# The last projection of 1024 tokens by Strassen's seven products, with the operand sums made during the gate stage

## The chip, the cores and the metric

The kernel runs on one core of one Trainium2 chip. The metric is the device time of one execution in microseconds (us). All runs told here are fast, at a granted TensorE clock of 0.996 to 1.0. In the profile lines PE is TensorE, PEld its weight loads, DVE VectorE, ACT ScalarE, POOL GpSimd and SPq the queue that issues the stores. PSUM is the memory of the tiles that matmuls write here, SBUF that of the other tiles in the kernel. A ratio of two kernels is the mean time of one kernel's fast runs over the mean of the other's of the same rounds, so it is not quite the ratio of the medians that are quoted.

Single executions of the same kernel here differ by up to 5 us. The text therefore uses a second measure, read from the traces: **the stage time, from the start of the first matmul of the second gate stage to the end of the span**. Everything that this study changes, but for a data type and the place of two loads of `x1` in the stages before, lies inside that stretch. The page gives spans to 0.1 us, so a difference of less than 0.1 us means nothing here.

## The reference

```python
def _B_ref(x, w_in, w_sp, b_sp, w_out):          # S = 2048 tokens, D = 1024, Fh = 1792
    z = gelu(einsum('bsd,df->bsf', x, w_in))
    z1 = z[..., :Fh]
    z2 = layernorm(z[..., Fh:])
    g = einsum('ts,bsf->btf', w_sp, z2) + b_sp[None, :, None]
    return einsum('bsf,fd->bsd', z1 * g, w_out)
...
h = layernorm(x) * (1 + ca) + sa
x = x + ga * attention(h)                        # "x1" in the kernel
h = layernorm(x) * (1 + cb) + sb
x = x + gb * _B_ref(h, ...)                      # the last line is what the change touches
```

The work at issue is `x1 + gb * ((z1 * g) @ w_out)` for the second 1024 tokens: a product of 1024 x 1792 with 1792 x 1024.

## The kernel before

Most large products of the kernel are already done by Strassen's scheme: a 2 x 2 block product in seven products instead of eight. A `Block` holds one such product. TensorE accumulates products 1, 6, 5 and 3 one after the other in the same PSUM bank `a`, and a "snap" of the running sum is taken before the next product is added. Products 2, 7 and 4 have the banks `c` and `b`.

```python
class Block:
    BANK = {1: "a", 6: "a", 5: "a", 3: "a", 2: "c", 7: "b", 4: "b"}
    ...
    def finish(self, n):
        ps = self.ps[self.BANK[n]]
        if n == 1:   self.s = self.snap(ps, 1)
        elif n == 2: self.out(1, 1, ps, self.s)
        elif n == 6: self.x = self.snap(ps, 2)
        elif n == 5: self.out(2, 2, self.ps["b"], self.snap(ps, 3))
        elif n == 3: self.out(1, 2, ps, None)
        elif n == 4: self.out(2, 1, ps, self.x)
        ...                                   # hooks: work to issue after product n

def steady(prev, blocks):                     # products 3 and 4 of a block run inside the next block
    for b in blocks:
        for n in (1, 2, 3, 6, 7, 4, 5):
            if n in (3, 4):
                prev and prev.run(n)
            else:
                b.run(n)
        prev = b
    return prev
```

The gate stage multiplies by `w_sp` in seven blocks for each half of the tokens, one for each pair of 128-feature groups. Its result `g` is multiplied into `z1T` by VectorE. The last projection is plain: 14 matmuls for each 128 tokens x 512 columns.

```python
def project(ti):
    ...
    cuts = (0, 512, D) if ti < NT - 1 else (0, 512, 768, 896, D)
    for c0, c1 in zip(cuts, cuts[1:]):
        bo = bank_ps("bo", [P, 512])[:, 0:c1 - c0]
        for f in range(NF):                                       # NF = 14
            nc.tensor.matmul(bo, z1T[ti // 8, f // 2][:, f % 2, t0:t0 + P],
                             wout[f // 2][:, f % 2, sl], start=(f == 0), stop=(f == NF - 1))
        nc.vector.tensor_mul(out=t, in0=bo, in1=late_gb[0][:, sl])
        nc.vector.tensor_add(out=outt[:, sl], in0=t, in1=x1rs[ti][:, sl])
        ...                                                       # store to the output
...
prev = steady(None, gates[1])        # the second gate stage
prev.run(3)
prev.run(4)
for ti in range(8, NT):              # the last projection
    project(ti)
```

The softmax here doesn't subtract the row's maximum and nothing guards it: scores larger than these inputs give would overflow.

Of the kernel before, what the change touches and what calls it, by code (L numbers as in the profile page):

```python
# [9 lines left out]
BF16 = mybir.dt.bfloat16  # L10
FP16 = mybir.dt.float16
# [5 lines left out]
def kernel(  # L17
# [16 lines left out]
    nc = tc.nc  # L34
    P = 128
    D = 1024
    S = 2048
    NT = 16
# [19 lines left out]
    def wide_ps(name, shape=(P, 1024), dtype=FP32):  # L58
        return psum.tile(list(shape), dtype, name=name, tag="wide", bufs=2)

    def bank_ps(name, shape, dtype=FP32):
        return psum.tile(shape, dtype, name=name, tag="bank", bufs=3)
# [23 lines left out]
    out_dram = out[0].rearrange("(tt p) d -> p tt d", p=P)  # L86
# [63 lines left out]
    cols = early.tile([P, 2, KD], FP32, name="cols")  # L150
# [234 lines left out]
    first = q_work(0, 0, bank_ps, outs)  # L385
# [56 lines left out]
    heap = Heap()  # L442
# [153 lines left out]
    for g, (i, kb) in enumerate(steps):  # L596
# [41 lines left out]
        n = (FILL if i else FILL0)[kb]  # L638
        if kb == 0:
            n = n if i + 1 < len(halves) else 1  # L640
# [3 lines left out]
            n = 0  # L644
        for j in range(2):
            nc.tensor.matmul(o_ps[j][:], vs[h][:, kb, :], pt[:, j * 512:(j + 1) * 512],  # L646
                             start=(kb == 0), stop=(kb == NKB - 1))
# [17 lines left out]
        elif kb == 14 and i + 2 == len(halves):  # L665
# [4 lines left out]
                stop=(k == 15), skip_group_check=True) for k in range(16)]  # L670
        if i + 1 == len(halves) or (i + 2 == len(halves) and kb >= 14):
            n = 1
# [20 lines left out]
    def scratch(name, shape, dtype=FP32):  # L693
        return scr.tile(shape, dtype, name=name, tag="k2", bufs=11)

    def short(name):
        return scr.tile([P, 512], FP16, name=name, tag="k1", bufs=6)
# [3 lines left out]
    def after(n, fn):  # L701

        later.append([n, fn])
# [54 lines left out]
    def steady(prev, blocks):  # L758
# [8 lines that stand above are left out]
# [28 lines left out]
    def copy_snap(ps, which):  # L795
        t = scratch("snap", [P, 512])[:, 0:ps.shape[1]]
        nc.scalar.activation(t, ps, ACT.Copy)  # L797
        return t

    def add_to(ps, snap):  # L800
        t = scratch("sum", [P, 512])[:, 0:ps.shape[1]]
        nc.vector.tensor_add(out=t, in0=ps, in1=snap)  # L802
        return t
# [171 lines left out]
    def h_op(c, m):  # L975
        return {1: hT[c, 0, 0], 2: hT[c, 0, 1], 4: hT[c, 1, 1], 3: hs[c][4], 5: hs[c][1],
                6: hs[c][2], 7: hs[c][3]}[m]
# [20 lines left out]
    w1, w1t, z1T = {}, {}, {}  # L998
# [51 lines left out]
    prev = steady(wos[3], wos[4:])  # L1050

    def gelu(dst, ps, snap):
        if snap is None:
            nc.scalar.activation(dst, ps, ACT.Gelu_apprx_tanh)
        else:
            t = add_to(ps, snap)
            after(2, lambda: nc.scalar.activation(dst, t, ACT.Gelu_apprx_tanh))
# [10 lines left out]
    def done_with_h(c):  # L1068
        users[c] -= 1
        if not users[c]:  # L1070
            heap.give(*(hT[c, i, j] for i in range(2) for j in range(2)),
                      *(hs[c][n] for n in (1, 2, 4)))
# [54 lines left out]
    def z1_block(c, p):  # L1127
        def operands(n):
            h = h_op(c, n)
            b = {1: (0, 0), 2: (1, 0), 3: (1, 1)}.get(n)  # L1130
            if b:
                w = [w1[c, p][:, 4 * b[0] + dc, b[1] * P:(b[1] + 1) * P] for dc in range(4)]
            else:
                w = [w1t[c, p][:, {4: 3, 5: 0, 6: 1, 7: 2}[n], dc, :] for dc in range(4)]
            return w, [h[:, dc, :] for dc in range(4)]

        def out(i, j, ps, snap):
            if (c, p) not in z1T:
                z1T[c, p] = heap.take("z1T", [P, 2, 1024], BF16)
            gelu(z1T[c, p][:, j - 1, (i - 1) * 512:i * 512], ps, snap)  # L1140

        b = Block(operands, copy_snap, out)
        b.on(3, lambda: done_with_h(c))
        return b
# [3 lines left out]
    NG = NF // 2  # L1148
    WQ = ((0, 1), (1, 1), (0, 0), (1, 0))
    W, wb, zr, zs, bb = {}, {}, {}, {}, {}  # L1150
# [55 lines left out]
    def zq(c, p, k, i):  # L1206
        return zr[c, p, k][:, :, i * P:(i + 1) * P]

    def z_sum(c, p, m):

        a11, a21, a12, a22 = (zq(c, p, k, i) for k in range(2) for i in range(2))
        if m == 1:
            zs[c, p] = heap.take("zs", [P, 2, 8, P], FP16)
            nc.vector.tensor_add(out=zs[c, p][:, 0], in0=a21, in1=a22)
        elif m == 2:
            nc.vector.tensor_sub(out=zs[c, p][:, 1], in0=zs[c, p][:, 0], in1=a11)
        elif m == 3:
            nc.vector.tensor_sub(out=a21, in0=a11, in1=a21)
        else:
            nc.vector.tensor_sub(out=a12, in0=a12, in1=zs[c, p][:, 1])  # L1220
# [3 lines left out]
    def work(n=1):  # L1224
        def go():
            for _ in range(n):
                if tasks:
                    tasks.pop(0)()
        return go
# [9 lines left out]
    for n, s in enumerate(seq):  # L1239
        b = z1b[n]  # L1240
# [29 lines left out]
    prev = dual(prev, order)  # L1270


    def plus(out, ps, other):
        nc.vector.scalar_tensor_tensor(out=out, in0=ps, scalar=DOWN, in1=other,  # L1274
                                       op0=ALU.mult, op1=ALU.add)

    def gate_block(c, p):
        def operands(n):
            if n in (5, 6):
                lhs = [zs[c, p][:, n - 5, k, :] for k in range(8)]  # L1280
            else:
                k_, i = {1: (0, 0), 7: (0, 1), 2: (1, 0), 3: (1, 0), 4: (1, 1)}[n]
                lhs = [zq(c, p, k_, i)[:, k, :] for k in range(8)]
            return lhs, [wb[n, k // 4][:, k % 4, :] for k in range(8)]

        def b(j):
            return bb[c][:, (j - 1) * 512:j * 512]

        def snap(ps, which):
            t = scratch("snap", [P, 512])  # L1290
            plus(t[:], ps, b({1: 1, 2: 1, 3: 2}[which]))
            return t[:]

        def out(i, j, ps, other):
            g = short("g").bitcast(BF16)
            plus(g[:], ps, b(2) if other is None else other)
            z = z1T[c, p][:, i - 1, (j - 1) * 512:j * 512]
            nc.vector.tensor_mul(out=z, in0=z, in1=g[:])

        g = Block(operands, snap, out)  # L1300
        g.on(2, lambda: z_sum(c, p, 4))
        g.on(7, lambda: heap.give(zr.pop((c, p, 0))))
        g.on(5, lambda: heap.give(zs.pop((c, p))))
        g.on(4, lambda: heap.give(zr.pop((c, p, 1))))
        if p + 1 < NG:
            g.on(1 if p else 2, lambda: norm_z(c, p + 1, 0))
            g.on(7, lambda: z_sum(c, p + 1, 1))
            g.on(5, lambda: z_sum(c, p + 1, 3), lambda: z_sum(c, p + 1, 2))
        if p + 2 < NG:
            g.on(7, lambda: load_z(c, p + 2, 0))  # L1310
            g.on(5, lambda: norm_z(c, p + 2, 1))
        if p + 3 < NG:
            g.on(4, lambda: load_z(c, p + 3, 1))
        return g

    wout, late_gb = {}, []
# [8 lines left out]
    x1rs = {}  # L1325

    def load_x1(ti):
        x1rs[ti] = scratch("x1r", [P, D], BF16)
        nc.sync.dma_start(x1rs[ti][:], x1_dram[ti])

    def project(ti):
        if ti + 2 < NT:
            load_x1(ti + 2)
        outt = scratch("outt", [P, D], BF16)
        cuts = (0, 512, D) if ti < NT - 1 else (0, 512, 768, 896, D)
        t0 = (ti % 8) * P
        for c0, c1 in zip(cuts, cuts[1:]):
            sl = slice(c0, c1)
            bo = bank_ps("bo", [P, 512])[:, 0:c1 - c0]
            for f in range(NF):  # L1340
                nc.tensor.matmul(bo, z1T[ti // 8, f // 2][:, f % 2, t0:t0 + P],  # L1341
                                 wout[f // 2][:, f % 2, sl], start=(f == 0),
                                 stop=(f == NF - 1))
            t = scratch("t", [P, 512])[:, 0:c1 - c0]
            nc.vector.tensor_mul(out=t, in0=bo, in1=late_gb[0][:, sl])  # L1345
            nc.vector.tensor_add(out=outt[:, sl], in0=t, in1=x1rs[ti][:, sl])
            if ti == NT - 1:
                nc.sync.dma_start(out_dram[:, ti, sl], outt[:, sl])
            work(2)()
        if ti < NT - 1:  # L1350
            nc.sync.dma_start(out_dram[:, ti, :], outt[:])

    gates = [[gate_block(c, p) for p in range(NG)] for c in range(2)]
    g = gates[0][0]
# [10 lines left out]
    prev = steady(g, gates[0][1:])  # L1365
# [25 lines left out]
    heap.give(*(z1T[0, p] for p in range(NG)))  # L1391
    for n in (1, 3, 2):
        z_sum(1, 0, n)
    prev = steady(None, gates[1])
    prev.run(3)
    prev.run(4)
    for ti in range(8, NT):
        project(ti)
    scr_pool.__exit__(None, None, None)
    heap_l.__exit__(None, None, None)  # L1400
    right.__exit__(None, None, None)
# [27 lines left out]
```

## Time and profile before

| | before |
|---|---|
| median of 3 runs | 1806.01 us (1805.94 to 1806.5) |
| TensorE busy | 1769.1 of 1804.9 us |
| second gate stage, about 1666 to 1751 us | TensorE 83.6, VectorE 61.1 us busy |
| last projection, 1753.05 to 1801.6 us | 224 matmuls of 512 columns, or their equal |
| last matmul to the end of the span | 3.28 us |
| stage time | 138.15 us |

From the page, the busy times of the engines and the chain of waits by engine: TensorE is the limit.

```profile
PE 1769.1 (98%) x8686; PEld 812.7 (45%) x8686; DVE 1478.9 (82%) x2518; ACT 1295.0 (72%) x1527; POOL 27.9 (2%) x39
...
PE 86%; DVE 8%; DMA 3%; issue 1%; ACT 1%; SPq 1%; POOL 0%; DVEq 0%; ACTq 0%; POOLq 0%
```

Busy time by stretch of the second gate stage and of the projection: the stretch, its length, then for each engine busy us and number of instructions, the granted clock, the share of the DMA engines, GB/s.

```profile
1666.00:1751.00 85.00, 83.63 (x388) 37.71 (x386) 61.11 (x104) 39.51 (x81) 0.00 (x0) 1.00 0.27 69
1751.00:1799.00 48.00, 48.00 (x227) 22.01 (x225) 22.04 (x33) 0.00 (x0) 0.00 (x0) 1.00 0.20 66
```

VectorE's timeline of one gate block (start, duration, engine, line, operation, output<-inputs, shapes; in brackets the idle time before, and what ended it). The lines are those before which VectorE stood idle. A block takes TensorE 12.09 us (56 matmuls of 0.216 us). In it VectorE waits 2.17 + 0.57 + 0.31 = 3.05 us. This idle time is what the change means to use.

```profile
1710.87 0.69 DVE L1274 SCALAR_TENSOR_TENSOR g<-cb,snap 128x512 bf16<-128x512 f32 x1 [2.17 <-PE cb L754]
...
1712.59 0.69 DVE L1274 SCALAR_TENSOR_TENSOR snap<-a,b_bc 128x512 f32<-128x512 f32 x1 [0.57 <-PE a L754]
...
1719.50 0.69 DVE L1274 SCALAR_TENSOR_TENSOR snap<-a,b_bc 128x512 f32<-128x512 f32 x1 [0.31 <-PE a L754]
```

TensorE's only wait after the stage has got going, before the last gate block's product 3:

```profile
1749.60 1.02 PE L754 MATMUL a<-w_16332,h_slots 128*128 128x512 f16 x4 [0.78 <-DVE snap L1274]
```

The end of the kernel, from the timelines of TensorE, VectorE and the store queue (SPq). The last matmul ends at 1801.62 and VectorE's last operation at 1802.28. The store is issued then, and the span ends at 1804.9.

```profile
1801.35 0.27 PE L1341 MATMUL bo<-w_out,h_slots 128*128 128x128 bf16 x2
...
1801.99 0.29 DVE L1346 TENSOR_TENSOR outt<-t,x1r 128x128 bf16<-128x128 f32 x1
...
1800.02 2.62 SPq L1348 DMA_DIRECT2D out_dram<-outt  x4
```

### The profile page before, as it was taken

The page shows a single profiled execution, that of the slowest core. Times are in us where ns is not written, and L with a number is a line of the kernel's source. Part 1 is how long each engine was busy: PE and PEld are TensorE (multiplying, and loading weights), DVE is VectorE, ACT ScalarE, POOL GpSimd, SP SyncE. Part 2 cuts the span into 40 slices and gives each one's busy share as a digit, 9 for nine tenths or more (in the row PEclk, how much of TensorE's full clock was granted, in tenths as well). Part 3 has the DMA queues.
Part 4 walks back from the last instruction along what each step waited for, and adds up shares of the span by engine and source line. Part 5 has one row for each costly group of instructions (what it writes and reads, how often), then busy time and mean ns, then how long its engine had stood idle before and what let it go on. Part 6 is the DMA issues. An engine that isn't in the chain of part 4 may idle for free.

```text
span 1804.9 us, 25203 instructions
## 1 busy us (share of the span) xinstructions
PE 1769.1 (98%) x8686; PEld 812.7 (45%) x8686; DVE 1478.9 (82%) x2518; ACT 1295.0 (72%) x1527; POOL 27.9 (2%) x39
## 2 busy tenths in 40 slices
PE   7999999999999999999999999999999999999999
PEld 4444444444444444444444444444444444444444
DVE  6998888888888888888899888976688688767764
ACT  6888999999899999999999999511335656634700
POOL 1000000000000000000000000000000000000000
PEclk9999999999999999999999999999999999999999
DMA  8584565555465345455546534453857364537402
GB/s 245 128 176 107 133 158 140 146 148 139 127 155 154 100 122 140 117 138 160 147 124 164 134 94 123 134 159 109 207 157 192 96 161 119 164 87 195 110 6 76
DMA packets 445202, 247.85 MB, mean 137 GB/s; under 512 B 289296, under 2 KB 406288, under 8 KB 445072
## 3 DMA queue, kind: packets, MB, share of 16 engines
q1 hardware_dynamic: 445072, 246.23, 52.2%
q8 instruction: 68, 1.11, 0.3%
q14 instruction: 62, 0.51, 0.1%
HBM read 144.18 MB, written 52.71 MB: 109 GB/s over the span
## 4 chain that ended last, share of the span: by engine, by line
PE 86%; DVE 8%; DMA 3%; issue 1%; ACT 1%; SPq 1%; POOL 0%; DVEq 0%; ACTq 0%; POOLq 0%
PE sps L377 23%; PE ops L646 23%; PE qps L356 12%; PE a L754 11%; PE cb L754 10%; PE bo L1341 5%; DVE sum L802 1%; DVE pacc L657 1%; DMA oq<-oT_dram 1%; DVE stats L136 1%; DMA wm<-in_w_mod_dram 1%; DVE z_st L1089 1%; DVE sum L875 0%; DVE x_in L876 0%; ACT snap L797 0%
## 5 line engine op out<-in xcount | busy, mean ns | idle before, releaser
L634 ACT ACTIVATE pt<-sps 128x1024 bf16<-128x1024 f32 x1024 | 1018.0, 1024 | 106.1 <-PE sps L377 73.8
L657 DVE TENSOR_TENSOR pacc<-pacc,pt 128x1024 bf16<-128x1024 bf16 x882 | 605.3, 686 | 59.0 <-ACT pt L634 1.6
L646 PE MATMUL ops<-pt,v_sb 128*128 128x512 bf16 x2048 | 609.9, 379 | 1.9 <-ACT pt L634 1.0
L377 PE MATMUL sps<-qT,kT 128*128 128x512 bf16 x2048 | 609.2, 379 | 1.3 <-ACT pt L634 0.9
L356 PE MATMUL qps<-h1T,wq_t 128*128 128x512 bf16 x992 | 335.8, 379 | 0.5 <-DVE rec L484 0.4
L646 PEld LDWEIGHTS <-v_sb 128*128 128x128 bf16 x2048 | 200.2, 98 | 243.1 <-issue 1.5
L377 PEld LDWEIGHTS <-kT 128*128 128x128 bf16 x2048 | 198.9, 98 | 243.9 <-issue 6.6
L356 PEld LDWEIGHTS <-wq_t 128*128 128x128 bf16 x992 | 97.0, 98 | 117.1
L797 ACT ACTIVATE snap<-a 128x512 f32<-128x512 f32 (+1 forms) x111 | 61.1, 564 | 115.2 <-PE a L754 107.5
L1203 ACT ACTIVATE zr<-zr,z_nm,z_rs 128x256 f16<-128x256 f16 x180 | 89.6, 585 | 74.8 <-DMA zr<-z_dram 69.7
L802 DVE TENSOR_TENSOR sum<-cb,snap 128x512 f32<-128x512 f32 (+1 forms) x114 | 74.2, 655 | 68.5 <-PE cb L754 40.4
L346 DVE CAST qT<-qps 128x512 bf16<-128x512 f32 x124 | 85.6, 691 | 40.2 <-PE qps L356 40.1
L754 PEld LDWEIGHTS <-h_slots 128*128 128x128 f16 (+1 forms) x544 | 53.2, 98 | 66.7 <-issue 6.4
L493 DVE TENSOR_TENSOR oT<-ou,rbc 128x1024 bf16<-128x1024 f32 x62 | 75.6, 1219 | 2.2 <-DMA rbc<-rec_dram 2.0
L754 PEld LDWEIGHTS <-zr 128*128 128x128 f16 x480 | 46.9, 98 | 57.6 <-issue 1.1
L754 PEld LDWEIGHTS <-oq 128*128 128x128 bf16 (+1 forms) x416 | 40.1, 98 | 56.3 <-DMA oq<-oT_dram 4.5
L471 DVE TENSOR_REDUCE den<-pT 128x8 f32<-128x1024 bf16 x54 | 63.9, 1183 | 0.0
L653 DVE COPY ou<-ops 128x512 f32<-128x512 f32 x63 | 43.5, 691 | 21.2 <-PE ops L646 21.2
L1341 PE MATMUL bo<-w_out,z1T 128*128 128x512 bf16 (+2 forms) x232 | 59.5, 372 | 0.0
L1274 DVE SCALAR_TENSOR_TENSOR g<-cb,snap 128x512 bf16<-128x512 f32 x42 | 29.0, 692 | 25.4 <-PE cb L754 23.5
L1345 DVE TENSOR_TENSOR t<-bo,gb 128x512 f32<-128x512 f32 (+2 forms) x34 | 22.4, 658 | 31.8 <-PE bo L1341 31.7
L1341 PE MATMUL bo<-w_out,h_slots 128*128 128x512 bf16 (+2 forms) x176 | 45.7, 360 | 0.0
(607 smaller groups left out, 1593.9 us busy)
## 6 DMA issues: line engine op xcount, KB each, us to landing
rbc<-rec_dram SPq DMA_DIRECT2D x63, 512.0 KB
v_sb<-in_A_v_cache_dram SPq DMA_DIRECT2D x40, 512.0 KB
oT_dram<-oT SPq DMA_DIRECT2D x62, 256.0 KB
sums_dram<-pacc SPq DMA_DIRECT2D x54, 256.0 KB
wm<-in_w_mod_dram SPq DMA_DIRECT2D x12, 1024.0 KB
zr<-z_dram SPq DMA_DIRECT2D x24, 512.0 KB
wo<-in_A_wo_dram SPq DMA_DIRECT2D x16, 512.0 KB
oq<-oT_dram SPq DMA_DIRECT2D x15, 512.0 KB
```

What stands on the lines that cost most here:

```text
L346: nc.vector.tensor_copy(out=out_t[:, sl], in_=box["ps"][:])
L356: nc.tensor.matmul(box["ps"][:], wq_t[:, dc, hc:hc + DH], src[:, dc, q0:q0 + 512], start=(n == 0), stop=(n == KD - 1))
L377: nc.tensor.matmul(sps[:, j * 512:(j + 1) * 512], kts[h][:, kb * P:(kb + 1) * P], qts[(h, qh)][:, j * 512:(j + 1) * 512], start=True, stop ...
L471: nc.vector.tensor_reduce(out=den[:], in_=state[i]["pT"][:], op=ALU.add, axis=mybir.AxisListType.X)
L493: nc.vector.tensor_mul(out=oT, in0=state[i]["ou"][:], in1=state[i]["rbc"][:])
L634: nc.scalar.activation(pt[:], s_tiles.pop(g)[:], ACT.Exp, scale=SCALE)
L646: nc.tensor.matmul(o_ps[j][:], vs[h][:, kb, :], pt[:, j * 512:(j + 1) * 512], start=(kb == 0), stop=(kb == NKB - 1))
L657: nc.vector.tensor_add(out=pacc[:], in0=pacc[:], in1=pt[:])
L754: nc.tensor.matmul(self.ps[self.BANK[n]], a, b, start=(n in (1, 2, 7) and k == 0), stop=(k == len(lhs) - 1), skip_group_check=True)
L802: nc.vector.tensor_add(out=t, in0=ps, in1=snap)
L1203: nc.scalar.activation(z, z, ACT.Identity, scale=z_rs[:, q:q + 1], bias=z_nm[:, q:q + 1])
L1341: nc.tensor.matmul(bo, z1T[ti // 8, f // 2][:, f % 2, t0:t0 + P], wout[f // 2][:, f % 2, sl], start=(f == 0), stop=(f == NF - 1))
```

## The change

The last projection of the second 1024 tokens becomes four `Block`s of seven products. Each takes 128 tokens of the first 512, 128 of the second 512, and the two column halves. The 28 operand sums that Strassen needs of `z1T` and the 28 of `w_out` are made by VectorE during the second gate stage, eight for each pair of feature groups. `z1T` becomes fp16. The fourth block has its own order: the products whose outputs need the most finishing come first, product 4 comes last and is split into 256, 128 and 128 columns, and seven elementwise operations go to GpSimd.

```diff
-                z1T[c, p] = heap.take("z1T", [P, 2, 1024], BF16)
+                z1T[c, p] = heap.take("z1T", [P, 2, 1024], FP16)
...
+    def p_sum(p, n):                      # four sums of z1T's quadrants, 128x512 each
+        ...
+        (nc.vector.tensor_add if n == 1 else nc.vector.tensor_sub)(out=t, in0=a, in1=b)
+    def wp_sum(p, n):                     # four of w_out's
+        ...
+        nc.vector.tensor_sub(out=t, in0=a, in1=b)
...
+    def proj_block(m):
+        ...
+        def out(i, j, ps, snap):
+            ...
+            t = scratch("sum", [P, 512])[:] if snap is None else add_to(ps, snap)
+            nc.vector.tensor_mul(out=t, in0=ps if snap is None else t, in1=gb[:, s0:s0 + 512])
+            nc.vector.tensor_add(out=o[:, s0:s0 + 512], in0=t, in1=x1[:, s0:s0 + 512])
...
+    def fold(eng, out, t, ti, s0):
+        eng.tensor_mul(out=t, in0=t, in1=late_gb[0][:, s0:s0 + 512])
+        eng.tensor_add(out=out, in0=t, in1=x1rs[ti][:, s0:s0 + 512])
+
+    def last_block(f, prev):
+        gb, dve, pool_ = late_gb[0], nc.vector, nc.gpsimd
+        ...
+        product(1, a);  s = copy_snap(a, 1)
+        prev.run(3)
+        product(6, a, first=False);  x = copy_snap(a, 2)
+        fold(pool_, x, x, 15, 0)
+        prev.run(4)
+        product(5, a, first=False);  u = copy_snap(a, 3)
+        fold(pool_, u, u, 15, 512)
+        product(7, b)
+        dve.tensor_mul(out=t[:], in0=b, in1=gb[:, 512:])
+        dve.tensor_add(out=o[:, 512:], in0=t[:], in1=u)
+        nc.sync.dma_start(out_dram[:, 15, 512:], o[:, 512:])
+        dve.tensor_mul(out=t[:], in0=b, in1=gb[:, 0:512])
+        dve.tensor_add(out=x, in0=t[:], in1=x)
+        product(2, c);  w = copy_snap(c, 0)
+        pool_.tensor_add(out=w, in0=w, in1=s)
+        fold(pool_, o11[:, 0:512], w, 11, 0)
+        nc.sync.dma_start(out_dram[:, 11, 0:512], o11[:, 0:512])
+        product(3, a, first=False)
+        dve.tensor_mul(out=t[:], in0=a, in1=gb[:, 512:])
+        dve.tensor_add(out=o11[:, 512:], in0=t[:], in1=x1rs[11][:, 512:])
+        nc.sync.dma_start(out_dram[:, 11, 512:], o11[:, 512:])
+        for c0, c1, new in ((0, 256, side_ps), (256, 384, bank_ps), (384, 512, wide_ps)):
+            ps = new("d", [P, c1 - c0])
+            product(4, ps[:], slice(c0, c1))
+            dve.tensor_mul(out=t, in0=ps[:], in1=gb[:, c0:c1])
+            dve.tensor_add(out=o[:, c0:c1], in0=t, in1=x[:, c0:c1])
+            nc.sync.dma_start(out_dram[:, 15, c0:c1], o[:, c0:c1])
...
+    for p in range(NG):                   # when the sums are issued
+        g = gates[1][p]
+        for n, k in ((2, 3), (6, 1), (7, 2), (5, 4)):
+            g.on(n, lambda p=p, k=k: wp_sum(p, k))
+        g.on(4, lambda p=p: p_sum(p, 1))
+        for n, k in ((1, 2), (2, 3), (3, 4)):
+            g.on(4, lambda p=p, n=n, k=k: after(n, lambda: p_sum(p, k)))
...
-    for ti in range(8, NT):
-        project(ti)
+    ...
+    prev = steady(f, projs[1:3])
+    last_block(projs[3], prev)
```

More of the change, by code (lines that the diff above doesn't have):

```diff
@@ L1294, in out @@
         def out(i, j, ps, other):
-            g = short("g").bitcast(BF16)
+            g = short("g")
             plus(g[:], ps, b(2) if other is None else other)
@@ L1331, in project @@
     def project(ti):
-        if ti + 2 < NT:
+        if ti + 2 < 8:
             load_x1(ti + 2)
         outt = scratch("outt", [P, D], BF16)
-        cuts = (0, 512, D) if ti < NT - 1 else (0, 512, 768, 896, D)
-        t0 = (ti % 8) * P
-        for c0, c1 in zip(cuts, cuts[1:]):
-            sl = slice(c0, c1)
-            bo = bank_ps("bo", [P, 512])[:, 0:c1 - c0]
+        for j in range(2):
+            sl = slice(j * 512, (j + 1) * 512)
+            bo = bank_ps("bo", [P, 512])[:]
             for f in range(NF):
-                nc.tensor.matmul(bo, z1T[ti // 8, f // 2][:, f % 2, t0:t0 + P],
+                nc.tensor.matmul(bo, z1T[0, f // 2][:, f % 2, ti * P:(ti + 1) * P],
@@ L1342, in project @@
                                  wout[f // 2][:, f % 2, sl], start=(f == 0),
                                  stop=(f == NF - 1))
-            t = scratch("t", [P, 512])[:, 0:c1 - c0]
+            t = scratch("t", [P, 512])[:]
             nc.vector.tensor_mul(out=t, in0=bo, in1=late_gb[0][:, sl])
             nc.vector.tensor_add(out=outt[:, sl], in0=t, in1=x1rs[ti][:, sl])
-            if ti == NT - 1:
-                nc.sync.dma_start(out_dram[:, ti, sl], outt[:, sl])
             work(2)()
-        if ti < NT - 1:
-            nc.sync.dma_start(out_dram[:, ti, :], outt[:])
+        nc.sync.dma_start(out_dram[:, ti, :], outt[:])
@@ new lines, with unit @@
+    units = []
+    def unit():
+        if not units:
+            t = heap.take("units", [P, 4, 512], FP16)
+            units.extend(t[:, k, :] for k in range(4))
+        return units.pop(0)
+    ps_, pt_ = {}, {}
+    def p_sum(p, n):
+        z = z1T[1, p]
+        a11, a21, a12, a22 = (z[:, k, i * 512:(i + 1) * 512] for k in range(2) for i in range(2))
+        t = ps_[p, n] = a21 if n == 3 else unit()
+        a, b = {1: (a21, a22), 2: (ps_.get((p, 1)), a11), 3: (a11, a21),
+                4: (a12, ps_.get((p, 2)))}[n]
+        (nc.vector.tensor_add if n == 1 else nc.vector.tensor_sub)(out=t, in0=a, in1=b)
@@ new lines, in wp_sum, with operands @@
+    def wp_sum(p, n):
+        b11, b12, b21, b22 = (wout[p][:, k, j * 512:(j + 1) * 512]
+                              for k in range(2) for j in range(2))
+        t = pt_[p, n] = b12.bitcast(FP16) if n == 1 else unit()
+        a, b = {3: (b22, b12), 1: (b12, b11), 2: (b22, pt_.get((p, 1))),
+                4: (b21, pt_.get((p, 2)))}[n]
+        nc.vector.tensor_sub(out=t, in0=a, in1=b)
+    outts = {}
+    def proj_block(m):
+        done = {1: 0, 2: 0}
+        def operands(n):
+            sl, ps = slice(m * P, (m + 1) * P), range(NG)
+            hi = slice(512 + m * P, 512 + (m + 1) * P)
+            a = {1: (0, sl), 2: (1, sl), 7: (0, hi), 4: (1, hi)}.get(n)
+            lhs = ([z1T[1, p][:, a[0], a[1]] for p in ps] if a else
+                   [ps_[p, {5: 1, 6: 2, 3: 4}[n]][:, sl] for p in ps])
+            b = {1: (0, 0), 2: (1, 0), 3: (1, 1)}.get(n)
+            rhs = ([wout[p][:, b[0], b[1] * 512:(b[1] + 1) * 512] for p in ps] if b else
+                   [pt_[p, {5: 1, 6: 2, 7: 3, 4: 4}[n]] for p in ps])
+            return lhs, rhs
+        def out(i, j, ps, snap):
+            ti, s0 = 8 + m + 4 * (i - 1), (j - 1) * 512
+            if not done[i]:
+                outts[ti] = scratch("outt", [P, D], BF16)
+            o, x1, gb = outts[ti], x1rs[ti], late_gb[0]
+            t = scratch("sum", [P, 512])[:] if snap is None else add_to(ps, snap)
+            nc.vector.tensor_mul(out=t, in0=ps if snap is None else t, in1=gb[:, s0:s0 + 512])
+            nc.vector.tensor_add(out=o[:, s0:s0 + 512], in0=t, in1=x1[:, s0:s0 + 512])
+            done[i] += 1
+            if done[i] == 2:
+                nc.sync.dma_start(out_dram[:, ti, :], o[:])
+        return Block(operands, copy_snap, out)
@@ new lines, in fold, with product @@
+    def fold(eng, out, t, ti, s0):
[3 more added lines that the diff above has]
+        gb, dve, pool_ = late_gb[0], nc.vector, nc.gpsimd
+        def product(n, bank, cols=slice(0, 512), first=True):
+            for k, (a, b) in enumerate(zip(*f.operands(n))):
+                nc.tensor.matmul(bank, a, b[:, cols], start=first and k == 0,
+                                 stop=(k == NG - 1), skip_group_check=True)
+        a, b = bank_ps("a", [P, 512])[:], wide_ps("b")[:, 0:512]
+        product(1, a)
+        s = copy_snap(a, 1)
+        prev.run(3)
+        product(6, a, first=False)
+        x = copy_snap(a, 2)
+        fold(pool_, x, x, 15, 0)
+        prev.run(4)
+        product(5, a, first=False)
+        u = copy_snap(a, 3)
+        fold(pool_, u, u, 15, 512)
+        product(7, b)
+        o11, o, t = (scratch("outt", [P, D], BF16), scratch("outt", [P, D], BF16),
+                     scratch("sum", [P, 512]))
+        dve.tensor_mul(out=t[:], in0=b, in1=gb[:, 512:])
+        dve.tensor_add(out=o[:, 512:], in0=t[:], in1=u)
+        nc.sync.dma_start(out_dram[:, 15, 512:], o[:, 512:])
+        t = scratch("sum", [P, 512])
+        dve.tensor_mul(out=t[:], in0=b, in1=gb[:, 0:512])
+        dve.tensor_add(out=x, in0=t[:], in1=x)
+        c = bank_ps("c", [P, 512])[:]
+        product(2, c)
+        w = copy_snap(c, 0)
+        pool_.tensor_add(out=w, in0=w, in1=s)
+        fold(pool_, o11[:, 0:512], w, 11, 0)
+        nc.sync.dma_start(out_dram[:, 11, 0:512], o11[:, 0:512])
+        product(3, a, first=False)
+        t = scratch("sum", [P, 512])
+        dve.tensor_mul(out=t[:], in0=a, in1=gb[:, 512:])
[4 more added lines that the diff above has]
+            product(4, ps[:], slice(c0, c1))
+            t = scratch("sum", [P, 512])[:, 0:c1 - c0]
+            dve.tensor_mul(out=t, in0=ps[:], in1=gb[:, c0:c1])
+            dve.tensor_add(out=o[:, c0:c1], in0=t, in1=x[:, c0:c1])
+            nc.sync.dma_start(out_dram[:, 15, c0:c1], o[:, c0:c1])
@@ L1393 @@
         z_sum(1, 0, n)
-    prev = steady(None, gates[1])
+    for p in range(NG):
[5 more added lines that the diff above has]
+            g.on(4, lambda p=p, n=n, k=k: after(n, lambda: p_sum(p, k)))
+    prev = steady(None, gates[1])
+    projs = [proj_block(m) for m in range(4)]
+    for m in range(4):
+        for n, k in ((6, 0), (7, 4)):
+            if m < 3:
+                projs[m].on(n, lambda k=k, m=m: load_x1(9 + m + k))
+    load_x1(8)
+    load_x1(12)
+    f = projs[0]
     prev.run(3)
+    f.run(1)
     prev.run(4)
-    for ti in range(8, NT):
-        project(ti)
+    heap.give(*(wb.pop((n, u)) for n in range(1, 8) for u in range(2)))
+    for n in (2, 6, 7, 5):
+        f.run(n)
+    prev = steady(f, projs[1:3])
+    last_block(projs[3], prev)
     scr_pool.__exit__(None, None, None)
```

## The prediction

> **What bounds the kernel.** The page: TensorE busy 1769.1 of 1804.9 us (98%) at full clock, 86% of the chain of waits. In the timeline a 512-column matmul starts every 0.216 us. The last projection runs 1753.05 to 1801.6 us without a gap; VectorE is then busy 22.0 of 48 us (busy time by stretch), ScalarE idle. From the end of the last matmul to the end of the span pass 3.3 us: VectorE 0.65, the last store 2.6. In the gate stage before it (1666 to 1751) VectorE is busy 61.1 of 85 us, TensorE 83.6.
>
> **Removed.** The last projection is 16 x 14 = 224 matmuls of 512 columns; Strassen's is 4 x 7 x 7 = 196. 28 x 0.216 = **6.05 us** leave TensorE, on the critical path.
>
> **Added in the gate stage.** 56 VectorE sums of 128x512, 16-bit. Like ones (the gate's multiply) take 0.43 us, 0.35 start to start, so 2.8-2.9 us for each gate block. A block costs VectorE 8.7-8.8 us now and TensorE 12.09; afterwards about 11.6. It still fits, barely: idle falls from some 3 us to 0.5 us a block, and the waits for snapshots move from the 3.5 us of slack that the product order gives to about 0.4 us of it. I expect 0 to 1 us of TensorE waits; the gap of 0.78 us before the last block's product 3 becomes about 1.1 us. Sum: +0.3 to 1.3 us.
>
> **Added in the projection.** A block: 49 matmuls, 10.6 us of TensorE; VectorE 11 operations at 0.69-0.72, 7.9 us; ScalarE 3 copies of 0.56. Fits, no waits.
>
> **The end.** Here the gain is partly given back. The last block puts seven fp32 128x512 operations on GpSimd. The trace of before shows GpSimd only with 1 and 16 columns, so its cost is an estimate: the Trainium skill, GPSIMD Engine Reference, "Elementwise — side-by-side cycle accounting", gives 4497 ns for 2048 fp32 elements, hence about 1.15-1.2 us for 512. VectorE waits for u's two operations, and the store of w's three precedes four others on the one store queue (0.33 us an issue). So VectorE ends about 2.6 us after the last matmul instead of 0.65: +2 us. The skill's SBUF — State Buffer, "SBUF: two separate sides", says that a VectorE operation with two SBUF inputs and a GpSimd operation exclude each other for a whole instruction. With that in force VectorE ends about 5.5 us after the last matmul: +4.9 us.  I take +3.3.
>
> **Sum.** 1806.0 - 6.05 + 0.8 + 3.3 = about **1804.0 us**; range 1801.3 to 1806.3. Chances: faster by over 2% 0.00, within 2% 0.99, slower 0.01 (2% is 36 us).
>
> **What will show it.**
> - TensorE: 28 fewer 512-column matmuls; last matmul about 1796.3.
> - Gate stage: VectorE 80 to 84 us busy in 85; TensorE's new waits for VectorE there under 1 us.
> - Tail: last matmul to the span's end 5.2 us if GpSimd takes 1.2 us and does not collide; 8 us if it does; GpSimd or VectorE's wait for it is then on the chain of waits, and VectorE operations with two SBUF inputs last or start over 1 us late beside GpSimd ones.
>
> **What would make it wrong.** VectorE saturated in the gate: z loads or ScalarE coming later (fewer free slots) push its in-order queue past 12.09 us a block, and the seven blocks lose over 3 us. GpSimd at 2 us or more for an operation: the tail costs over 6 us and the change is no gain. Or GpSimd off the critical path: a tail of +1, and 1801.

## The result and the profile after

| | before | after |
|---|---|---|
| median, first set of rounds | 1805.97 us (4 runs) | 1803.53 us (4 runs) |
| ratio, 95% interval | | 0.9988 (0.9971 to 1.0005) |
| stage time | 138.15 us | 136.24 us |
| its start to the end of the last matmul | 134.87 us | 129.22 us |
| last matmul to VectorE's last operation | 0.66 us | 3.88 us |
| last matmul to the end of the span | 3.28 us | 7.02 us |

By the whole time alone no gain is shown in these rounds, since the interval of the ratio includes 1. By the stage time the change is worth 1.9 us. TensorE finishes 5.65 us earlier, and 3.74 us of that is given back after its last matmul.

From the page of the changed kernel:

```profile
PE 1756.4 (97%) x8517; PEld 809.1 (45%) x8644; DVE 1505.5 (83%) x2583; ACT 1303.7 (72%) x1540; POOL 37.8 (2%) x46
...
PE 84%; DVE 9%; DMA 4%; issue 2%; ACT 1%; SPq 0%; POOL 0%; DVEq 0%; ACTq 0%; POOLq 0%
```

Some matmul records are missing from a trace, so the weight loads (PEld) are the better count: 42 fewer. The kernel before issues 252 matmuls for the projection, 15 output halves of 14 and the last one as three pieces of 14. The changed one issues 210, 27 products of 7 and the last one as three pieces of 7.

Busy time by stretch, as before:

```profile
1666.00:1751.00 85.00, 83.50 (x387) 37.65 (x385) 76.71 (x154) 39.94 (x81) 0.00 (x0) 1.00 0.27 75
1751.00:1797.00 46.00, 44.97 (x218) 20.88 (x220) 33.02 (x51) 7.76 (x13) 8.26 (x6) 1.00 0.17 60
```

VectorE has 50 more operations in the gate stage and 15.6 us more busy time, and TensorE is as busy as before. VectorE's timeline shows one wait in a gate block, 0.61 us, where it had three that made 3.05:

```profile
1711.08 0.69 DVE L1274 SCALAR_TENSOR_TENSOR g<-cb,snap 128x512 f16<-128x512 f32 x1 [0.62 <-PE cb L754]
...
1723.16 0.69 DVE L1274 SCALAR_TENSOR_TENSOR g<-cb,snap 128x512 f16<-128x512 f32 x1 [0.61 <-PE cb L754]
```

TensorE has no new wait in the gate stage. The old one grew from 0.78 to 0.91 us:

```profile
1749.94 1.02 PE L754 MATMUL a<-w_16332,zr 128*128 128x512 f16 x4 [0.91 <-DVE snap L1274]
```

It has two short new waits just after the stage, in the first projection block, both for VectorE's work on the last pair of feature groups. The matmul at 1756.31 starts 0.33 us after the one before it instead of 0.22, when the last multiplication by `g` (L1298) is done. The one at 1759.49 starts 0.37 us after the one before it, when the first of the two sums at 1759.02, of 0.42 us, is done. Together that is 0.27 us:

```profile
1756.31 0.39 PE L754 MATMUL cb<-w_out,h_slots 128*128 128x512 bf16 x1
...
1759.49 0.39 PE L754 MATMUL cb<-units,h_slots 128*128 128x512 f16 x1
```

```profile
1755.82 0.42 DVE L1298 TENSOR_TENSOR h_slots<-h_slots,g 128x512 f16<-128x512 f16 x1
...
1759.02 0.75 DVE L1367 TENSOR_TENSOR h_slots<-h_slots 128x512 f16<-128x512 f16 x2
```

The tail is where the gain goes. The timelines of TensorE's last matmul, VectorE, GpSimd (POOL) and the store queue follow:

```profile
1795.96 0.22 PE L1420 MATMUL d<-units,h_slots 128*128 128x128 f16 x1
```

```profile
1788.62 0.69 DVE L802 TENSOR_TENSOR sum<-cb,snap 128x512 f32<-128x512 f32 x1 [1.60 <-PE cb L754]
1789.35 1.48 DVE L1400 TENSOR_TENSOR sum<-sum,gb 128x512 f32<-128x512 f32 x1
1790.87 1.76 DVE L1401 TENSOR_TENSOR outt<-sum,x1r 128x512 bf16<-128x512 f32 x1
...
1793.67 0.69 DVE L1438 TENSOR_TENSOR outt<-sum,snap 128x512 bf16<-128x512 f32 x1 [0.45 <-POOL snap L1411]
...
1795.00 1.04 DVE L1442 TENSOR_TENSOR snap<-sum,snap 128x512 f32<-128x512 f32 x1
1795.96 0.68 DVE L1451 TENSOR_TENSOR sum<-a,gb 128x512 f32<-128x512 f32 x1
1796.67 1.04 DVE L1452 TENSOR_TENSOR outt<-sum,x1r 128x512 bf16<-128x512 f32 x1
...
1798.08 0.92 DVE L1459 TENSOR_TENSOR outt<-sum,snap 128x256 bf16<-128x256 f32 x1
...
1799.77 0.29 DVE L1459 TENSOR_TENSOR outt<-sum,snap 128x128 bf16<-128x128 f32 x1
```

```profile
1787.79 1.27 POOL L1410 TENSOR_TENSOR snap<-snap,gb 128x512 f32<-128x512 f32 x1 [272.62 <-ACT snap L797]
1789.13 1.15 POOL L1411 TENSOR_TENSOR snap<-snap,x1r 128x512 f32<-128x512 f32 x1
1790.81 1.27 POOL L1410 TENSOR_TENSOR snap<-snap,gb 128x512 f32<-128x512 f32 x1 [0.52 <-ACT snap L797]
1792.16 1.48 POOL L1411 TENSOR_TENSOR snap<-snap,x1r 128x512 f32<-128x512 f32 x1
1793.83 1.66 POOL L1446 TENSOR_TENSOR snap<-snap 128x512 f32<-128x512 f32 x1 [0.19 <-ACT snap L797]
1795.57 1.59 POOL L1410 TENSOR_TENSOR snap<-snap,gb 128x512 f32<-128x512 f32 x1
1797.24 1.48 POOL L1411 TENSOR_TENSOR outt<-snap,x1r 128x512 bf16<-128x512 f32 x1
```

```profile
1794.39 0.33 SPq L1439 DMA_DIRECT2D out_dram<-outt  x1
1798.75 0.33 SPq L1448 DMA_DIRECT2D out_dram<-outt  x1
1799.17 0.38 SPq L1453 DMA_DIRECT2D out_dram<-outt  x1
1799.65 1.37 SPq L1460 DMA_DIRECT2D out_dram<-outt  x3
```

Read VectorE and GpSimd side by side. VectorE's operations with one input in PSUM (L802, L1451) keep their 0.69 us while GpSimd runs. Four of those with both inputs in SBUF and 512 columns do not, and each of the four ends 0.55 us after a GpSimd operation ends. GpSimd ends at 1790.28 and L1400 at 1790.83. The same pairs follow at 1792.08 and 1792.63, at 1795.49 and 1796.04, and at 1797.16 and 1797.71. A fifth, of 256 columns, takes 0.92 us, where before the change such an operation took 0.43; it ends 0.28 us after GpSimd's last. The exception is L1438: it starts at 1793.67 while GpSimd is idle, and keeps its 0.69. Four of GpSimd's own seven operations grow too, from 1.15 and 1.27 to between 1.48 and 1.66 us; one of them starts at 1793.83, during L1438.

The store queue shows a second loss. The store of GpSimd's last result (L1448) waits until 1798.75, and the store behind it, whose data VectorE had ready at 1797.71, goes out at 1799.17. A store takes the queue 0.33 to 0.40 us. The last one goes out only at 1800.6, though its data was ready at 1800.06. Of the 3.74 us that the tail grew, 3.22 are VectorE's later end (3.88 against 0.66 us after the last matmul), and the other 0.52 come behind it, with the stores.

### The profile page after: what moved, and what is told of

Its sections match the earlier page's. It is cut to its first block, busy times and chain, and to the rows that moved or that the text cites. A ratio compares the mean times of both kernels' runs of the same rounds, so it can differ in the third digit from the quotient of the medians.

```text
span 1803.2 us, 25116 instructions
## 1 busy us (share of the span) xinstructions
PE 1756.4 (97%) x8517; PEld 809.1 (45%) x8644; DVE 1505.5 (83%) x2583; ACT 1303.7 (72%) x1540; POOL 37.8 (2%) x46
## 4 chain that ended last, share of the span: by engine, by line
PE 84%; DVE 9%; DMA 4%; issue 2%; ACT 1%; SPq 0%; POOL 0%; DVEq 0%; ACTq 0%; POOLq 0%
PE ops L646 23%; PE sps L377 22%; PE a L754 12%; PE qps L356 12%; PE cb L754 11%; PE bo L1339 2%; DMA oq<-oT_dram 1%; DVE pacc L657 1%; DVE sum L802 1%; DVE stats L136 1%; DMA wm<-in_w_mod_dram 1%; DVE z_st L1089 1%; PE mps L183 0%; DMA w_15467<-in_B_w_in_dram 0%; ACT snap L797 0%
## 5 line engine op out<-in xcount | busy, mean ns | idle before, releaser
L634 ACT ACTIVATE pt<-sps 128x1024 bf16<-128x1024 f32 x1024 | 1018.6, 1024 | 105.3 <-PE sps L377 71.0
L646 PE MATMUL ops<-pt,v_sb 128*128 128x512 bf16 x1992 | 597.4, 379 | 6.6 <-DVE ou L653 1.1
L377 PE MATMUL sps<-qT,kT 128*128 128x512 bf16 x2000 | 598.6, 379 | 1.4 <-ACT pt L634 0.9
L797 ACT ACTIVATE snap<-a 128x512 f32<-128x512 f32 (+1 forms) x123 | 68.3, 568 | 172.3 <-PE a L754 132.0
L1203 ACT ACTIVATE zr<-zr,z_nm,z_rs 128x256 f16<-128x256 f16 x188 | 93.6, 586 | 91.9 <-DMA zr<-z_dram 91.9
L802 DVE TENSOR_TENSOR sum<-cb,snap 128x512 f32<-128x512 f32 (+1 forms) x123 | 80.4, 658 | 77.2 <-PE cb L754 47.4
L653 DVE COPY ou<-ops 128x512 f32<-128x512 f32 x63 | 43.5, 691 | 21.2 <-PE ops L646 21.2
L130 POOL TENSOR_TENSOR rstd<-var,neg_half 128x1 f32<-128x1 f32 x30 | 22.5, 751 | 1328.1 <-DVE var L128 1291.6
L655 DVE TENSOR_TENSOR pacc<-pt 128x1024 bf16<-128x1024 bf16 x63 | 43.0, 682 | 2.4 <-ACT pt L634 2.4
L1274 DVE SCALAR_TENSOR_TENSOR g<-cb,snap 128x512 f16<-128x512 f32 x42 | 29.0, 691 | 17.7 <-PE cb L754 16.4
L660 DVE COPY ou<-ops 128x512 f32<-128x512 f32 x63 | 43.1, 684 | 0.0
```

The lines of the kernel that those rows point to most:

```text
L377: nc.tensor.matmul(sps[:, j * 512:(j + 1) * 512], kts[h][:, kb * P:(kb + 1) * P], qts[(h, qh)][:, j * 512:(j + 1) * 512], start=True, stop ...
L634: nc.scalar.activation(pt[:], s_tiles.pop(g)[:], ACT.Exp, scale=SCALE)
L646: nc.tensor.matmul(o_ps[j][:], vs[h][:, kb, :], pt[:, j * 512:(j + 1) * 512], start=(kb == 0), stop=(kb == NKB - 1))
L797: nc.scalar.activation(t, ps, ACT.Copy)
L802: nc.vector.tensor_add(out=t, in0=ps, in1=snap)
L1203: nc.scalar.activation(z, z, ACT.Identity, scale=z_rs[:, q:q + 1], bias=z_nm[:, q:q + 1])
```

## The experiments

Theory 1: TensorE's 6 us are real and the sums are free. The loss is in the tail, because GpSimd and two-SBUF-input operations of VectorE exclude each other and because the stores queue up behind GpSimd. Rivals: (a) the nearly full VectorE costs time in the gate stage; (b) the tail belongs to any Strassen block, and the reordered block is the best end; (c) GpSimd is merely slow.

Eight runs. The stage time is the measure, and the medians are of rounds with the kernel before on the same chip.

| run | stage time, us | start to last matmul's end | last matmul to the end | median (before) |
|---|---|---|---|---|
| before | 138.15 | 134.87 | 3.28 | |
| after | 136.24 | 129.22 | 7.02 | 1803.53 (1805.97) |
| after_again | 136.22 | 129.22 | 7.00 | 1803.14 (1805.55) |
| plain_end | 135.39 | 130.03 | 5.36 | 1802.57 (1805.55) |
| psum_place | 135.17 | 129.22 | 5.95 | 1802.22 (1805.55) |
| no_sums | 135.92 | 128.92 | 7.00 | 1802.84 (1805.55) |
| store_act | 135.61 | 129.21 | 6.40 | 1802.56 (1804.75) |
| dve_all | 135.97 | 129.20 | 6.77 | 1804.18 (1804.75) |
| sums_twice | 149.57 | 142.52 | 7.05 | 1815.68 (1804.75) |
| combined | 133.94 | 129.20 | 4.74 | 1801.26 (1804.75) |

### after_again: the changed kernel unaltered

> The changed kernel unaltered, timed with the others on one chip. Both theories: 2.4 us (0.13%) under the kernel before, give or take 1 us; last matmul about 5.4 us earlier than before's, tail from the last matmul to the end about 7 us against 3.3.

Measured: ratio 0.9987 (0.9974 to 0.9999), stage time 136.22 us, tail 7.00 us. The stage time repeats to 0.02 us.

### no_sums: what do the sums cost?

```diff
-                   [ps_[p, {5: 1, 6: 2, 3: 4}[n]][:, sl] for p in ps])
+                   [z1T[1, p][:, 0, sl] for p in ps])
...
-                   [pt_[p, {5: 1, 6: 2, 7: 3, 4: 4}[n]] for p in ps])
+                   [wout[p][:, 0, 0:512] for p in ps])
...
-        for n, k in ((2, 3), (6, 1), (7, 2), (5, 4)):
-            g.on(n, lambda p=p, k=k: wp_sum(p, k))
-        ...                                            # and the p_sum hooks
```

> Wrong result on purpose: the 56 operand sums are left out and the products read other tiles of the same shape, so TensorE's work is the same. Theory 1 (the sums hide in VectorE's idle time): 0 to 0.5 us under the changed kernel; the gap before the gate's last product 3 goes from 0.91 back to 0.78 us. Rival (part of the missing 3.6 us is lost to a saturated VectorE in the gate stage): 1 us or more under it.

Its output is wrong, which doesn't matter for the time. The stage time falls by 0.30 us, and the gap before the last product 3 is back at 0.78 us. So 56 VectorE operations cost 0.3 us together: rival (a) falls. The trace shows where: of TensorE's waits, 0.13 us of the gap before product 3 and the one of about 0.15 us for a sum in the first projection block are gone; the other one there, for the multiplication by `g`, stays.

### sums_twice: how near is the limit?

```diff
-        (nc.vector.tensor_add if n == 1 else nc.vector.tensor_sub)(out=t, in0=a, in1=b)
+        for _ in range(1 if n == 3 else 2):
+            (nc.vector.tensor_add if n == 1 else nc.vector.tensor_sub)(out=t, in0=a, in1=b)
...
-        nc.vector.tensor_sub(out=t, in0=a, in1=b)
+        for _ in range(1 if n == 1 else 2):
+            nc.vector.tensor_sub(out=t, in0=a, in1=b)
```

> Six of the eight operand sums of every gate block are computed twice, which changes no value: 2.1 us more of VectorE a block. The trace shows 0.61 us of VectorE idle in a steady block of 12.09 us. Theory 1 (the sums nearly fill VectorE and are free only just): a block becomes about 13.5 us, 8 to 10 us in all, second gate stage to end about 145 us. Rival (there is plenty of room, the sums are nowhere near a limit): under 2 us in all.

Measured: 13.3 us longer, more than expected. TensorE's timeline shows a wait in every steady block, and the block takes 14.12 us instead of 12.09:

```profile
1708.80 1.89 PE L754 MATMUL a<-w_t,zs 128*128 128x512 f16 x8 [1.88 <-DVE snap L1274]
...
1722.92 1.45 PE L754 MATMUL a<-w_t,zs 128*128 128x512 f16 x6 [1.88 <-DVE snap L1274]
```

The size was off because a repeated sum follows an operation that writes the same tile. A pair lasts 0.87 to 0.88 us in the trace, so the second adds about 0.44 us, not the 0.35 of an independent one. Six of them make 2.64 us, and 12.09 - 0.61 + 2.64 = 14.12. The point stands: eight sums a block fit, with 0.6 us to spare, and of the 2.64 us added here all that exceeded this showed in TensorE's period.

### plain_end: the fourth block in the ordinary order

```diff
-    prev = steady(f, projs[1:3])
-    last_block(projs[3], prev)
+    prev = steady(f, projs[1:])
+    prev.run(3)
+    prev.run(4)
```

> The fourth projection block in the ordinary product order, its sums on VectorE and ScalarE only, no GpSimd, no split last product. Theory 1 (the tail loss is made by GpSimd and VectorE excluding each other): laid out from the trace's durations the end comes about 1 us EARLIER than the changed kernel's, 0.5 to 1.5 us; last matmul 0.7 us later, tail 5 to 6 us. Rival (the reordering is worth what it was written for, and any Strassen block must end with such a tail): 1 us or more LATER than the changed kernel.

Measured: 0.84 us shorter than the changed kernel. The last matmul comes 0.81 us later (TensorE waits 0.69 us for the last snap), and the tail is 1.65 us shorter. The specially ordered block, as the changed kernel has it, is thus worse than the ordinary one. (This run takes away the order, the split of product 4 and GpSimd all at once.) Of rival (b) only the second half falls, and only for this version of the order: the ordinary Strassen block too has a tail 2.08 us longer than the kernel before, and once its two faults are cured (`combined`, below) the reordered end is 1.45 us shorter than this one.

### psum_place: the same operations without a second SBUF input

```diff
-        dve.tensor_mul(out=t[:], in0=b, in1=gb[:, 512:])
-        dve.tensor_add(out=o[:, 512:], in0=t[:], in1=u)
+        dve.tensor_mul(out=b2, in0=b, in1=gb[:, 512:])      # b2: free half of b's PSUM tile
+        dve.tensor_add(out=o[:, 512:], in0=b2, in1=u)
...
-            dve.tensor_mul(out=t, in0=ps[:], in1=gb[:, c0:c1])
-            dve.tensor_add(out=o[:, c0:c1], in0=t, in1=x[:, c0:c1])
+            dve.tensor_mul(out=ps[:], in0=ps[:], in1=gb[:, c0:c1])
+            dve.tensor_add(out=o[:, c0:c1], in0=ps[:], in1=x[:, c0:c1])
```

The other products of the block, and product 4 of the block before it, are changed in the same way.

> In the last block, and in the one output of the block before it that meets GpSimd, VectorE writes its products in place into PSUM, so that no VectorE operation there reads two SBUF operands; same operations, same order, same GpSimd work. Theory 1: VectorE operations go from 1.04-1.76 us back to 0.69, GpSimd's from 1.5-1.66 to 1.15-1.27; the tail shrinks from 7.0 to about 5 us, total 1.5 to 2.5 us under the changed kernel. Rival (GpSimd is just slow, and the tail is its length plus the order of the stores): durations on GpSimd stay, total within 0.5 us of the changed kernel.

The durations are just those that theory 1 gave. VectorE's and GpSimd's timelines:

```profile
1786.93 0.70 DVE L1404 TENSOR_TENSOR cb<-cb,gb 128x512 f32<-128x512 f32 x1
1787.66 0.69 DVE L1405 TENSOR_TENSOR outt<-cb,x1r 128x512 bf16<-128x512 f32 x1
...
1793.70 0.69 DVE L1454 TENSOR_TENSOR outt<-a,x1r 128x512 bf16<-128x512 f32 x1
```

```profile
1789.72 1.15 POOL L1415 TENSOR_TENSOR snap<-snap,x1r 128x512 f32<-128x512 f32 x1
1791.40 1.27 POOL L1449 TENSOR_TENSOR snap<-snap 128x512 f32<-128x512 f32 x1 [0.53 <-ACT snap L797]
1792.75 1.27 POOL L1414 TENSOR_TENSOR snap<-snap,gb 128x512 f32<-128x512 f32 x1
```

The operations that took 1.48, 1.76 and 1.04 us take 0.69 to 0.70, and all of GpSimd's are at 1.15 or 1.27. Rival (c) falls: the exclusion is real. But the time falls by only 1.07 us, not 1.5 to 2.5. VectorE ends 1.38 us earlier, and then the store queue shows. The store that waits for GpSimd goes out at 1795.28, those behind it at 1795.70 and from 1796.17 on, and the end keeps 0.3 us less of the gain than VectorE does.

### store_act: one store on another queue

```diff
-        nc.sync.dma_start(out_dram[:, 11, 0:512], o11[:, 0:512])
+        nc.scalar.dma_start(out_dram[:, 11, 0:512], o11[:, 0:512])
```

> Only the store that waits for GpSimd's last result goes to ScalarE's queue instead of the common store queue, so that the four later stores need not stand behind it. The trace of the changed kernel has them issued at 1799.17 and three from 1799.7 to 1801.0, though VectorE had the first ready at 1797.7 and the next at 1799.0. If the queue order costs the tail: from the start of the second gate stage to the end 135.7 us instead of 136.23 (-0.3 to -0.7). If not: 136.2.

Measured: 0.63 us shorter, with VectorE and GpSimd unaltered. The store queue's timeline now follows VectorE instead of GpSimd, whose last result comes at 1795.54:

```profile
1794.56 0.33 SPq L1453 DMA_DIRECT2D out_dram<-outt  x1
1795.85 1.39 SPq L1460 DMA_DIRECT2D out_dram<-outt  x3
```

### dve_all: the seven operations on VectorE

```diff
-        gb, dve, pool_ = late_gb[0], nc.vector, nc.gpsimd
+        gb, dve, pool_ = late_gb[0], nc.vector, nc.vector
```

> The last block's seven GpSimd operations on VectorE, at 0.69-0.72 us each, in the same places. If GpSimd was a real relief of VectorE: laid out by hand VectorE ends 1 us later, second gate stage to end 136.8 us (+0.3 to +1.5). If the exclusion had eaten all of the relief: 136.2 or less.

Measured: the stage time is 0.27 us shorter than with GpSimd, so my layout by hand, which said longer, missed. Without the exclusion VectorE does its own operations at 0.69 us, and the seven more keep it busy without a break from 1788.2 to 1799.6. But the run changes two things. VectorE itself ends 4.24 us after the last matmul, 0.36 us later than in the changed kernel; the time is shorter because no store waits for GpSimd any more (the last one goes out 0.02 us after its data is ready, against 0.58). Against `store_act`, which cures the stores and keeps GpSimd, this run is 0.36 us longer. So GpSimd did relieve VectorE, by 0.36 us only, and the order of its store cost more than that.

### combined: both cures

As in psum_place, and the two column halves of product 7 in the other order, because GpSimd finishes `x` before `u`. Two stores go to ScalarE's queue:

```diff
+        dve.tensor_mul(out=b2, in0=b, in1=gb[:, 0:512])
+        dve.tensor_add(out=x, in0=b2, in1=x)
+        dve.tensor_mul(out=b, in0=b, in1=gb[:, 512:])
+        dve.tensor_add(out=o[:, 512:], in0=b, in1=u)
...
+        nc.scalar.dma_start(out_dram[:, 11, 0:512], o11[:, 0:512])
...
+            (nc.scalar if c0 == 256 else nc.sync).dma_start(out_dram[:, 15, c0:c1], o[:, c0:c1])
```

> Both cures together: products scaled in place in PSUM, the two column halves of product 7 taken in the order in which GpSimd has their addends ready, and two of the stores on ScalarE's queue. By the durations of the run with PSUM in place VectorE ends 0.5 to 0.7 us earlier than there and no store waits for GpSimd: second gate stage to end 134.0 to 134.6 us against 136.23 (and 138.15 before), so 1.6 to 2.2 us under the changed kernel.

Measured: correct, stage time 133.94 us, a little better than the range given: 2.3 us under the changed kernel and 4.2 under the one before. The median is 1801.26 us against 1804.75, ratio 0.998 (0.9968 to 0.9993). It is the best version. How much of it is the swap of the two halves was not run apart. VectorE ends 1.77 us after the last matmul, where the kernel before needed 0.66.

## Why the prediction was right

The time was 1804.0 us, with a range of 1801.3 to 1806.3; 1803.53 was measured. Term by term:

- **Removed matmuls.** Predicted -6.05 us. The last matmul's end comes 5.65 us earlier in the stage. The 0.40 us between are the next term.
- **Losses on TensorE.** Predicted +0.3 to 1.3 us, entered as +0.8. Measured 0.40: 0.13 is the gap of 0.78 that became 0.91 (I had said 1.1), and the other 0.27 are the two waits in the first projection block. There the prediction said "Fits, no waits", which was wrong by this much. The sums account for 0.30 of the 0.40 by no_sums. No steady gate block waits for VectorE.
- **VectorE's room in the gate.** Predicted idle time 3 us a block down to 0.5; measured 3.05 to 0.61. The busy time of the stage was predicted at 80 to 84 us and is 76.7. That was too high, since only 50 of the 56 sums fall into the stretch and each adds 0.31 us of busy time, not 0.35.
- **GpSimd's duration.** Predicted 1.15 to 1.2 us for 512 fp32 elements, an estimate from the Trainium skill, GPSIMD Engine Reference, section "Elementwise — side-by-side cycle accounting". Undisturbed it takes 1.15 us for the add of `x1`, whose second input is bf16, and 1.27 us for the multiply and for the add of two fp32 tiles, so the trace agrees to within 0.1 us.
- **The exclusion.** It was left open in the prediction whether it would bite. It does: the Trainium skill, SBUF — State Buffer, section "SBUF: two separate sides", states it, and this trace agrees, with 0.69 against 1.04 to 1.76 us on VectorE and psum_place as the test. GpSimd stood on the chain of waits, as forecast: two of its operations, from 1790.81 to 1793.64, and then VectorE to the end.
- **The tail.** Entered as +3.3, between +2 (no collision) and +4.9 (collision). Measured +3.74 with collision. The term of the collision was over-sized: VectorE was to end 5.5 us after the last matmul and ended 3.88 after it. The term without it was right: 2.6 us were predicted, and psum_place, which takes the collision away, shows 2.51. So the collision was put at 2.9 us and is worth 1.37. What VectorE does not explain, the wait of stores behind GpSimd's, was under-sized: the tail without collision was to be 5.2 us and is 5.95 in psum_place. Its parts by experiment: 1.07 for the exclusion as the changed kernel stands (psum_place), 0.63 for the store order (store_act), 2.28 for the two with the swapped halves (combined). That leaves 1.46 for the work that is still behind the last matmul.

The sum came out closer than its parts, because +0.8 was too much by 0.4 and +3.3 too little by 0.44. That is luck in part: +3.3 lies between the two cases and forecasts neither. With the collision, which is what happened, the terms add up to 1806.0 - 6.05 + 0.8 + 4.9 = 1805.65 us, 2.1 us over the measured time. The mechanism, TensorE's gain and the signs of all terms were right; that the number came within 0.5 us is owed to the compromise, and the interval of the measured ratio is some 6 us wide.

What stays open: the spread of single runs. It lies ahead of the second gate stage, whose start varies from 1663.8 to 1667.0 us in these profiles, and was not traced further. What the swap of the halves adds in combined was not separated either.

## What to carry to other kernels

When TensorE is the limit and another engine idles for 3 us in each 12, work may be added to it almost for nothing: here 2.4 us in each block cost 0.3 us in all, because VectorE's queue stayed under the period. Measure how near the limit is by doubling the work. The end of the kernel was the exception: there little was hidden, so count what remains behind the last matmul, and look at each queue in order, stores too. Before work goes to GpSimd beside VectorE, look at how many inputs VectorE's operations take from SBUF; leaving one of them in PSUM kept the two engines apart here.

## What the Trainium skill lacked or had wrong

- SBUF — State Buffer: it tells of the exclusion, but not what a held VectorE operation still costs. Here it ends 0.55 us after the GpSimd operation ends, in four cases out of four with 512 columns, instead of taking its full 0.69 us, and 0.28 us after it in the one case with 256.
- SBUF — State Buffer: it says which operations do not contend, but for authors it gives no remedy other than the schedule. Writing a product back into its PSUM bank, so that the next operation has only one SBUF input, took both engines back to their undisturbed durations (0.69 to 0.70 us, 1.15 to 1.27 us).
- GPSIMD Engine Reference: its comparison has only an add of 2048 elements at 1.96 times VectorE's time. At 512 elements these runs show 1.15 to 1.27 us against 0.69, 1.7 to 1.8 times. The shorter time is that of the adds with a bf16 input; the multiplies and the add with fp32 inputs alone take 1.27.
- DMA: Bandwidth & Descriptors: it says that issuing from several engines saves only the time that the sequencer takes to initiate the DMA. A store holds its queue for 0.33 to 0.40 us here, but moving the one store that waited for GpSimd to another queue was worth 0.63 us: the stores behind it no longer waited for its data.
